# Thirty-two rows of wq through GpSimd in four transfers, each behind a quarter of gate_w, and thirty-two as quarter rows

## The chip, the cores and the metric

The kernel runs on one core of one Trainium2 chip. The metric is the device time of one execution in microseconds (us), as the median of several runs. The core has five engines with queues of their own: TensorE (PE in the profile), VectorE (DVE), ScalarE (ACT), GpSimd (POOL) and SyncE (SP), which here only issues transfers. Transfers between HBM and the on-chip memory (SBUF) are carried by 16 DMA engines, whichever engine has issued them.

## The reference, cut to what matters

Eight rows `x` (8 x 576) go through cached attention and through a small MLP, and a gate mixes the two results.

```python
def reference(A_x, A_k_cache, A_v_cache, A_wq, A_wo, B_x, B_w1, B_b1, B_w2, B_b2, gate_w):
    x = A_x                                                     # 8 x 1 x 576
    g = sigmoid((x * gate_w).sum(-1, keepdims=True))
    q = (x @ A_wq).reshape(8, 1, 32, 128)                       # A_wq is 576 x 4096
    p = softmax(q . k_cache * 128**-0.5)                        # k_cache, v_cache: 8 x 32 x 4096 x 128
    a = (p @ v_cache) @ A_wo                                    # A_wo is 4096 x 576
    b = gelu(layernorm(x) @ B_w1 + B_b1) @ B_w2 + B_b2          # B_w1 is 576 x 4608
    return g * a + (1 - g) * b
```

All operands are bf16. The two caches are 537 MB together, all of the weights some 20 MB.

## The kernel before, in words

There are 32 turns `n`, one for each batch row and group of eight heads. A turn loads 8.4 MB of keys (`load_k`, L328) and 8.4 MB of values (`load_v`, L339); each of the 128 partitions gets one run of 64 KB. VectorE multiplies the keys with the broadcast query (L500), TensorE sums the products (L511 and L183, the helper `held`), VectorE finishes the sums (L523), then come the softmax and the product with the values (L564).

An instruction is recorded by `op` or `aside` in a list for its engine, and the order of these lists is the order of execution on each engine. Waits are on semaphores. `load` (its DMA is recorded at L287) gives every transfer a semaphore of its own, on the queue of the engine that is named. Nothing plans the order: it is written out by hand.

The order of SP's queue is what sets the order of the transfers: rows 0 to 511 of `wq` (4096 KB, four rows to a partition, 32 KB each), rows 512 to 575 of `wq` as 128 half rows of 4 KB (512 KB), the first keys in two halves, `w1` in two parts, `w2` (which waits for the last matmul of the queries, `p_Q`, since it goes into the place of `wq`), the keys of turn 1 (which wait for VectorE to be done with half of turn 0's keys and for `p_up`), the values of turn 0 in two parts, and from there keys and values in turn; at the end come `wo` and the last values in pieces. ACT's queue carries `x`, `gate_w` (to eight partitions, 1152 bytes each), `b1` and `b2`. GpSimd issues no transfer: it begins with the identity matrix `ident` (L365, L368), then fills `xz`, `yz`, `ones`, `mA` and `shift`.

What happens ahead of the first turn is a small chain of its own. VectorE first makes `own`, `fine` and `shift` from `ident`, then the statistics of `x` (L397 to L405), then the dot product with `gate_w` (L407). ACT blanks three banks of PSUM (L378, for which it waits for `mA`), makes `sel_f` and `Sel` from `ident` (L390, L392), the square root (L409) and the sigmoid of the gate (L410), and spreads the last 64 columns of `x` into `xz` (L416, L417). TensorE transposes `x` (L424, six small matmuls), VectorE copies the result (L429); the same follows for the normalised `y`. Then TensorE computes the queries: two halves by four head groups by `NKT` = 5 matmuls, 40 in all (L451), for which it waits for both transfers of `wq`. ACT takes the queries out of PSUM (L454), they are broadcast (L465, L469) and turn 0's query is scaled down to its tile (L475).

The functions below are `spread`, `transposed` and `untransposed`, which the change rewrites, and the statements around them.

Of the kernel before, what the change touches and what calls it, by code (L numbers as in the profile page):

```python
# [6 lines left out]
ACT = mybir.ActivationFunctionType  # L7
ALU = mybir.AluOpType
# [4 lines left out]
B = 8  # L13
D = 576
H = 32
DH = 128
SK = 4096
F = 4608
NKF = 4
NKT = NKF + 1  # L20
# [21 lines left out]
class Stream:  # L42
# [102 lines left out]
def bass_gated_mix__mha_block_cached__mixer_channel_mlp__decode_kernel(  # L145
# [18 lines left out]
    op = S.op  # L164

    def aside(engine, fn, waits=()):
        return op(engine, fn, waits, side=1)

    def pstride(t):
        return t[tuple([slice(None)] * len(t.shape))].ap[0][0]  # L170

    def view(t, offset, shape):
        ap = []
        stride = 1
        for n in reversed(shape[1:]):
# [17 lines left out]
    KR = sb("KR", [128, RB0 + 9 * F // 2], BF16)  # L193
    VB = sb("VB", [128, NTT, DH], BF16)
    wq_sb = view(VB, 0, [128, 4, SK])
    wq_t = view(VB, 4 * SK, [128, SK // 2])
    w1_sb = view(KR, RB0, [128, 4, F])
    w1_t = view(KR, RB0 + 4 * F, [128, F // 2])
    V_AHEAD = 88
# [3 lines left out]
    p1 = sb("p1", [128, 2, CT, DH], BF16)  # L203
# [14 lines left out]
    xz = early([B, 2, 64, 2])  # L218
    yz = early([B, 2, 64, 2])
    xT_sb = early([128, NKF + 2, B])  # L220
# [52 lines left out]
    tr_ps = bank[0:2]  # L273
# [3 lines left out]
    up_ps = bank[6]  # L277
    y_ps = bank[7]
    up_bank = (qb_ps, *tr_ps)
    YT_COL = 64  # L280

    sK = nc.alloc_semaphore("sK")
    sV = nc.alloc_semaphore("sV")
# [2 lines left out]
    def load(engine, dst, src, name, waits=()):  # L286
        return op(engine, lambda e: e.dma_start(dst, src), waits, dma=(nc.alloc_semaphore(name), 16))  # L287
# [2 lines left out]
    x_flat = A_x.rearrange("b s d -> (b s) d")  # L290
    out_flat = out.rearrange("b s d -> (b s) d")

    def bcast(t):
        return bass.AP(tensor=t.tensor, offset=t.offset, ap=[[0, B], [1, D]])
# [12 lines left out]


    def kv_src(cache, n):
# [54 lines left out]
    def memset(engine, ap, value):  # L364
        return op(engine, lambda e: e.memset(ap, value))  # L365

    c_id0 = memset("gpsimd", ident[:], 0.0)
    c_id = op("gpsimd", lambda e: e.affine_select(out=ident[:], in_=ident[:], compare_op=ALU.not_equal, fill=1.0,  # L368
                                                  base=0, pattern=[[-1, 128]], channel_multiplier=1), [c_id0])
# [35 lines left out]
    t_vpe = op("vector", lambda e: e.tensor_scalar(out=stat[:, 4:5], in0=stat[:, 6:7], scalar1=1e-5, scalar2=None,  # L405
                                                   op0=ALU.add), [t])
    t_gs = op("vector", lambda e: e.tensor_tensor_reduce(out=junk, in0=x_sb, in1=gw8, scale=1.0, scalar=0.0,  # L407
                                                         op0=ALU.mult, op1=ALU.add, accum_out=stat[:, 8:9]), [ld_gw, t1])
    a_sqrt = aside("scalar", lambda e: e.activation(out=stat[:, 5:6], in_=stat[:, 4:5], func=ACT.Sqrt), [t_vpe])  # L409
    a_g = aside("scalar", lambda e: e.activation(out=stat[:, 9:10], in_=stat[:, 8:9], func=ACT.Sigmoid), [t_gs])  # L410
    G_COL, OMG_COL = 9, 10


    def spread(dst, src, waits):

        aside("scalar", lambda e: e.activation(out=dst[:, 0, :, 0], in_=src[:, 512:576], func=ACT.Copy), [*waits, c_z])  # L416
        return aside("scalar", lambda e: e.activation(out=dst[:, 1, :, 1], in_=src[:, 512:576], func=ACT.Copy))  # L417

    def transposed(src, srcz, col, waits):
        last = None  # L420
        for kt in range(NKF + 2):
            o = up_ps[:, col + kt * B:col + (kt + 1) * B]
            i = src[:, kt:NKF * 128:NKF] if kt < NKF else srcz[:, kt - NKF, :, :].rearrange("b r s -> b (r s)")
            last = aside("tensor", lambda e, o=o, i=i: e.matmul(o, lhsT=i, rhs=ident[0:B, 0:B], start=True, stop=True),  # L424
                      waits if kt == 0 else ())
        return last

    def untransposed(dst, col, waits):
        return op("vector", lambda e: e.tensor_copy(  # L429
            out=dst.rearrange("p k b -> p (k b)"), in_=up_ps[:, col:col + (NKF + 2) * B]), waits)  # L430

    v_xz = spread(xz, x_sb, [ld_x])
    p_xT = transposed(x_sb, xz, 0, [ld_x, c_id, v_xz])
    v_xT = untransposed(xT_sb, 0, [p_xT])
# [4 lines left out]
    p_yT = transposed(y_sb, yz, YT_COL, [v_yz, v_xT])  # L439
    v_yT = untransposed(yT_sb[:, :, :], YT_COL, [p_yT])  # L440

    a_Q = []
    p_Q = None
    for half in range(2):
        for h in range(4):
            for kt in range(NKT):
                o = tr_ps[half][32 * h:32 * h + B, :]
                at = (kt * SK + half * (SK // 2) if kt < NKF else NKF * SK) + h * DH
                r = bass.AP(tensor=VB, offset=at, ap=[[pstride(VB), 128], [4 * DH, 4], [1, DH]])
                xi = kt if kt < NKF else NKF + half  # L450
                p_Q = aside("tensor", lambda e, o=o, r=r, kt=kt, xi=xi: e.matmul(  # L451
                    o, lhsT=xT_sb[:, xi, :], rhs=r, start=(kt == 0), stop=(kt == NKT - 1)),
                    [v_xT, *ld_wq, *c_ps] if h == kt == half == 0 else ())
        a_Q.append(aside("scalar", lambda e, half=half: e.activation(  # L454
            out=Q4[:, half * 512:(half + 1) * 512], in_=tr_ps[half][:, :], func=ACT.Copy, scale=inv_sqrt_dh), [p_Q]))
# [443 lines left out]
```

## Time and profile before

| | |
|---|---|
| median of 3 runs | 1295.06 us (1294.94 to 1295.06) |
| span of the profiled execution, first to last instruction | 1293.1 us |
| its own time | not given apart from the span; the median is 1.96 us above the span |
| read from HBM | 556.95 MB, 431 GB/s over the span |
| busy: PE, DVE, ACT, POOL | 731.3, 851.9, 73.2, 12.7 us |
| mean granted TensorE clock | 0.837 |

Times in the profile are counted from the first instruction. A line of the chain of waits gives start, length and what ran or was waited for. A line of the timeline gives start, length, engine, source line, operation, tiles, shapes and count; in brackets stands how long the engine had been idle and what ended that. A line of the DMA issues gives the number of such issues, the size of each and the median time from issue to landing. A row of the table by windows gives, for each stretch, the busy time of the five engines with their number of instructions, the granted clock, the busy share of the 16 DMA engines and the rate in GB/s; a packet counts in the stretch in which it starts, so short stretches can show a share over one.

### The profile page before, as it was taken

The numbers are of one execution on the slowest core, as the hardware profiler recorded it, in microseconds if no ns is written. First come the engines' busy times: TensorE is split into PE (matmuls) and PEld (weight loads), VectorE is DVE, ScalarE is ACT, GpSimd is POOL, SyncE is SP. The second block draws the span as 40 slices with busy tenths as digits, with TensorE's granted clock in tenths as the row PEclk, the third lists the DMA queues.
The fourth block names the chain that finished last, engine by engine and source line by source line (L and its number), as shares of the span: only waits on it lengthen the run. The fifth ranks groups of instructions, "written<-read, shape, count | busy, mean of one in ns | idle before, by whom it ended". The sixth has DMA issues, their size and how long they took to land.

```text
span 1293.1 us, 10903 instructions
## 1 busy us (share of the span) xinstructions
PE 731.3 (57%) x4824; PEld 142.8 (11%) x3032; DVE 851.9 (66%) x1078; ACT 73.2 (6%) x164; POOL 12.7 (1%) x23
## 2 busy tenths in 40 slices
PE   3755566455556555556555556555556555557556
PEld 0211111011111011111011111001111001111003
DVE  3646667766667766667766667766668766667763
ACT  3300000000000000000000000000000000000001
POOL 0100000000000000000000000000000000000001
PEclk8978888877898787799778888877888877798878
DMA  9999999999999999999999999999999999999998
GB/s 405 427 447 424 430 442 430 438 432 430 442 428 428 444 426 430 444 428 438 434 428 442 428 428 444 428 428 444 428 438 434 428 442 428 428 444 428 428 438 356
DMA packets 11728, 557.07 MB, mean 431 GB/s; under 512 B 1448, under 2 KB 1608, under 8 KB 2120
## 3 DMA queue, kind: packets, MB, share of 16 engines
q1 hardware_dynamic: 11520, 556.93, 99.7%
q8 instruction: 5, 0.08, 0.0%
q10 hardware_dynamic: 200, 0.03, 0.0%
q14 instruction: 3, 0.02, 0.0%
HBM read 556.95 MB, written 0.01 MB: 431 GB/s over the span
## 4 chain that ended last, share of the span: by engine, by line
DMA 67%; DVE 18%; PE 9%; issue 5%; DVEq 1%; SPq 0%
DMA KR<-in_A_k_cache_dram 66%; DVE p L500 15%; PE psb L183 7%; DVE s_sb L523 2%; DMA KR<-in_A_wo_dram 2%; PE psb L511 2%; DVEq L523 0%; DVEq L137 0%; SPq L287 0%; PE psb L754 0%; DVE p L850 0%; DVEq L500 0%
## 5 line engine op out<-in xcount | busy, mean ns | idle before, releaser
L500 DVE TENSOR_TENSOR p<-KR,q_n 128x4096 bf16<-128x4096 bf16 x256 | 581.6, 2282 | 213.6 <-DMA KR<-in_A_k_cache_dram 213.6
L183 PE MATMUL psb<-p,ident 128*128 128x512 bf16 x1792 | 483.8, 415 | 0.0
L511 PE MATMUL psb<-p,ident 128*128 128x512 bf16 x256 | 112.1, 438 | 511.6 <-DVE p L500 511.6
L523 DVE TENSOR_REDUCE s_sb<-psb 128x512 f32 (+1 forms) x256 | 175.3, 685 | 106.9 <-PE psb L183 60.4
L511 PEld LDWEIGHTS psb<-p,ident 128*128 128x128 bf16 x256 | 26.1, 102 | 964.3 <-DVE p L500 963.8
L564 PE MATMUL psb<-VB,P 128*32 128x512 bf16 x1984 | 112.7, 380 | 0.0
L552 DVE TENSOR_SCALAR P<-E,own 128x256 bf16<-128x256 bf16 x256 | 53.1, 282 | 87.4 <-ACT E L549 87.4
L475 ACT ACTIVATE q_n<-q_bc 128x128 bf16<-128x128 bf16 x32 | 9.9, 310 | 871.3 <-DVE p L500 871.3
L564 PEld LDWEIGHTS psb<-VB,P 128*32 128x32 bf16 x1984 | 50.1, 97 | 47.9
L581 PE MATMUL psb<-selO,O_sb 128*128 128x8 f32 x256 | 33.9, 259 | 22.5 <-ACT O_sb L576 22.5
L581 PEld LDWEIGHTS psb<-selO,O_sb 128*128 128x128 f32 x256 | 31.0, 191 | 38.3 <-ACT O_sb L576 38.3
L576 ACT ACTIVATE O_sb<-psb 128x512 f32<-128x512 f32 x32 | 19.1, 597 | 197.9 <-PE psb L564 197.9
L571 PEld LDWEIGHTS psb<-rs,ones 128*128 128x128 f32 x64 | 12.1, 190 | 46.6 <-issue 44.4
L691 POOL TENSOR_TENSOR p<-OT_sb,fine 128x512 bf16<-128x512 bf16 (+1 forms) x4 | 5.0, 1278 | 1196.8 <-PE psb L571 1193.0
L549 ACT ACTIVATE E<-s_sb,mD 128x256 bf16<-128x256 f32 x32 | 16.0, 499 | 0.0
L540 DVE TENSOR_REDUCE mA<-s_sb 128x1 f32<-128x256 f32 x32 | 13.5, 420 | 1.1
L480 ACT ACTIVATE OT_sb<-O_n,G 128x8 bf16<-128x8 f32 x31 | 9.3, 301 | 84.3 <-DVE O_n L587 84.3
L555 DVE TENSOR_REDUCE es<-E 128x1 f32<-128x256 bf16 x32 | 13.2, 412 | 0.0
L571 PE MATMUL psb<-rs,ones 128*128 128x8 f32 x64 | 9.2, 216 | 1.3 <-DVE O_n L587 1.3
L653 PE MATMUL psb<-VB,hT_sb 128*8 128x288 bf16 x72 | 6.5, 358 | 4.7 <-POOL hT_sb L632 4.7
L556 DVE TENSOR_SCALAR rs<-own,es 128x8 f32<-128x8 f32 x32 | 7.4, 231 | 1.1
L548 DVE STREAM_TRANSPOSE mD<-mC 128x32 f32<-128x32 f32 x32 | 6.8, 212 | 1.1
(98 smaller groups left out, 125.8 us busy)
## 6 DMA issues: line engine op xcount, KB each, us to landing
KR<-in_A_k_cache_dram SPq DMA_DIRECT2D x2, 4096.0 KB, 27.2
VB<-in_A_v_cache_dram SPq DMA_DIRECT2D x1, 5376.0 KB, 27.1
VB<-in_B_w_dram SPq DMA_DIRECT2D x1, 5184.0 KB, 40.6
KR<-in_B_w_dram SPq DMA_DIRECT2D x1, 4608.0 KB, 43.2
VB<-in_A_wq_dram SPq DMA_DIRECT2D x1, 4096.0 KB, 12.5
KR<-in_A_v_cache_dram SPq DMA_DIRECT2D x1, 4096.0 KB, 22.3
VB<-in_A_v_cache_dram SPq DMA_DIRECT2D x1, 2816.0 KB, 38.4
KR<-in_A_wo_dram SPq DMA_DIRECT2D x1, 2304.0 KB, 20.7
```

What stands on the lines that cost most here:

```text
L183: return e.add_instruction(mybir.InstMatmult(name=nc.get_next_instruction_name(), engine=mybir.EngineType.PE, ins=[e.lower_ap(rhs), e.lowe ...
L500: v_mult[n, c] = op("vector", lambda e: e.tensor_tensor(out=p1[:, par, :, :], in0=k_of(), in1=qb, op=ALU.mult), [k_land[n, s], a_q[n], p_s ...
L511: fn = lambda e, r=r: e.matmul(tr_ps[par][:, :], lhsT=ident[:, :], rhs=r, start=True, stop=False)
L523: v_red[n, c] = op("vector", lambda e: e.tensor_reduce(out=s_of(), in_=tr_ps[par][:, :].rearrange("p (t c) -> p t c", c=CH), axis=AX.X, op ...
L540: t = op("vector", lambda e: e.tensor_reduce(out=mA[:, 0:1], in_=s_sb[:, :], axis=AX.X, op=ALU.max), [v_red[n, NC - 1], c_mA])
L549: a_exp[n] = op("scalar", lambda e: e.activation(out=E[:, :], in_=s_sb[:, :], func=ACT.Exp, bias=mD[:, 0:1], scale=1.0), [v_nm[n], v_P.get ...
L552: v_P[n] = op("vector", lambda e, h=h: e.tensor_scalar(out=P[:, :, h, :], in0=E[:, :].rearrange("p (q t) -> p q t", t=TQ), scalar1=own[:, ...
L555: t = op("vector", lambda e: e.tensor_reduce(out=es[:, :], in_=E[:, :], axis=AX.X, op=ALU.add), [a_exp[n]])
L564: p_pv[n] = op("tensor", lambda e, o=o, tq=tq, at=at, v=v: e.matmul(o, lhsT=P[:, tq, :, :].rearrange("p h t -> p (h t)"), rhs=v.rearrange( ...
L571: p_z[n] = op("tensor", lambda e: e.matmul(oz_ps[:, HB:2 * HB], lhsT=ones[:, :], rhs=rs[:, :], start=True, stop=True), [v_rs[n], v_norm.ge ...
L576: a_ev[n] = op("scalar", lambda e: e.activation(out=O_sb[:].rearrange("p t d -> p (t d)"), in_=o_ps[n // last][:, :], func=ACT.Copy), [p_p ...
L581: p_oz[n] = op("tensor", lambda e, tt=tt: e.matmul(o, lhsT=O_sb[:, tt, :], rhs=selO[:, tt, :], start=(tt == 0), stop=(tt == TQ - 1 and stop)),
```

## The change

Of the last 64 rows of `wq`, 32 stay on SP's queue, now as 128 quarter rows of 2 KB (`XQ` = 4, 256 KB). The other 32 (256 KB) go on GpSimd's queue in four transfers of 8 rows; a row is two pieces of 4 KB, which lie 64 elements apart in `VB` so that they stay two, and the 32 rows land in partitions 64 to 95 (transfer `j` in partitions 64 + j, 68 + j, ... 92 + j). Ahead of each of the four stands a quarter of `gate_w`, broadcast to eight partitions in two pieces of 144 bytes each, also on GpSimd's queue; ACT no longer loads `gate_w`. GpSimd issues the eight transfers after filling `mA` and before it makes `ident`.

The queries take 56 matmuls in place of 40: four of 512 columns as before, two of 256 columns for the quarter rows, and one of 512 columns over 32 partitions for the rows that GpSimd brought. The transposition of `x` has nine matmuls in place of six. The dot product with `gate_w` and its sigmoid come after the transposition of `y`; before, they came ahead of the transposition of `x`.

```diff
     wq_sb = view(VB, 0, [128, 4, SK])
-    wq_t = view(VB, 4 * SK, [128, SK // 2])
+    XQ = 4
+    XR = 64 // 2
+    XP = 64
+    wq_t = view(VB, 4 * SK, [128, SK // XQ])
+    WQB = 4 * SK + SK // XQ
+    WQH = SK // 2 + 64
...
-    gw8 = early([B, D])
+    GW = D // 8
+    gw8 = early([B, 8, GW + 8])
...
-    ld_gw = load("scalar", gw8, bcast(gate_w), "ld_gw")
...
     ld_wq = [load("sync", wq_sb, A_wq[0:512, :].rearrange("(p kt) n -> p kt n", kt=4), "ld_wqa"),
-             load("sync", wq_t, halves(A_wq), "ld_wqb")]
+             load("sync", wq_t, A_wq[512:512 + XR, :].rearrange("r (s n) -> (r s) n", s=XQ), "ld_wqb")]
...
+    c_mA = memset("gpsimd", mA[:], 0.0)
+    ld_gw = []
+    for j in range(4):
+        ld_gw.append(load("gpsimd", gw8[:, 2 * j:2 * j + 2, 0:GW],
+                          bass.AP(tensor=gate_w.tensor, offset=gate_w.offset + 2 * j * GW, ap=[[0, B], [GW, 2], [1, GW]]), f"ld_gw{j}"))
+        ld_wq.append(load(
+            "gpsimd", bass.AP(tensor=VB, offset=(XP + j) * pstride(VB) + WQB, ap=[[4 * pstride(VB), 8], [WQH, 2], [1, SK // 2]]),
+            bass.AP(tensor=A_wq.tensor, offset=A_wq.offset + (512 + XR + j) * SK, ap=[[4 * SK, 8], [SK // 2, 2], [1, SK // 2]]), f"ld_wqc{j}"))
     c_id0 = memset("gpsimd", ident[:], 0.0)
...
-    c_mA = memset("gpsimd", mA[:], 0.0)
...
+    def spread_x(waits):
+        def into(at, ap):
+            return bass.AP(tensor=xz.tensor, offset=xz.offset + at, ap=[[pstride(p1), B]] + ap)
+        xr = x_sb[:, 512:512 + XR]
+        aside("scalar", lambda e: e.activation(
+            out=into(0, [[129, XQ], [XQ, XR]]),
+            in_=bass.AP(tensor=xr.tensor, offset=xr.offset, ap=[[pstride(p1), B], [0, XQ], [1, XR]]), func=ACT.Copy), [*waits, c_z])
+        return aside("scalar", lambda e: e.activation(out=into(XQ * 128 + XP, [[1, XR]]), in_=x_sb[:, 512 + XR:576], func=ACT.Copy))
...
-            for kt in range(NKT):
-                o = tr_ps[half][32 * h:32 * h + B, :]
-                at = (kt * SK + half * (SK // 2) if kt < NKF else NKF * SK) + h * DH
-                r = bass.AP(tensor=VB, offset=at, ap=[[pstride(VB), 128], [4 * DH, 4], [1, DH]])
+            r0 = 32 * h
+            for kt in range(NKF + 3):
+                if kt < NKF:
+                    at, p0, p1_, g, o0, xi = kt * SK + half * (SK // 2), 0, 128, 4, 0, kt
+                elif kt < NKF + 2:
+                    at, p0, p1_, g, o0, xi = NKF * SK, 0, 128, 2, (kt - NKF) * 2 * DH, 2 * half + kt
+                else:
+                    at, p0, p1_, g, o0, xi = WQB + half * WQH, XP, XP + XR, 4, 0, NKF + XQ
```

More of the change, by code (lines that the diff above doesn't have):

```diff
@@ L279, in bass_gated_mix__mha_block_cached__mixer_channel_mlp__decode_kernel @@
     up_bank = (qb_ps, *tr_ps)
-    YT_COL = 64
+    YT_COL = 128
     sK = nc.alloc_semaphore("sK")
@@ L417, in spread @@
         return aside("scalar", lambda e: e.activation(out=dst[:, 1, :, 1], in_=src[:, 512:576], func=ACT.Copy))
+    def spread_x(waits):
[6 more added lines that the diff above has]
+        return aside("scalar", lambda e: e.activation(out=into(XQ * 128 + XP, [[1, XR]]), in_=x_sb[:, 512 + XR:576], func=ACT.Copy))
     def transposed(src, srcz, col, waits):
         last = None
-        for kt in range(NKF + 2):
+        n = NKF + len(srcz)
+        for kt in range(n):
             o = up_ps[:, col + kt * B:col + (kt + 1) * B]
-            i = src[:, kt:NKF * 128:NKF] if kt < NKF else srcz[:, kt - NKF, :, :].rearrange("b r s -> b (r s)")
+            i = src[:, kt:NKF * 128:NKF] if kt < NKF else srcz[kt - NKF]
             last = aside("tensor", lambda e, o=o, i=i: e.matmul(o, lhsT=i, rhs=ident[0:B, 0:B], start=True, stop=True),
@@ L426, in transposed, with untransposed @@
         return last
-    def untransposed(dst, col, waits):
+    def untransposed(dst, col, n, waits):
         return op("vector", lambda e: e.tensor_copy(
[L430 to L434, printed above, removed]
+            out=dst.rearrange("p k b -> p (k b)"), in_=up_ps[:, col:col + n * B]), waits)
+    v_xz = spread_x([ld_x])
+    p_xT = transposed(x_sb, [xz[:, i, :] for i in range(XQ + 1)], 0, [ld_x, c_id, v_xz])
+    v_xT = untransposed(xT_sb, 0, NKF + XQ + 1, [p_xT])
     t = op("vector", lambda e: e.reciprocal(out=stat[:, 7:8], in_=stat[:, 5:6]), [a_sqrt])
@@ L438, in bass_gated_mix__mha_block_cached__mixer_channel_mlp__decode_kernel @@
     v_yz = spread(yz, y_sb, [v_y])
-    p_yT = transposed(y_sb, yz, YT_COL, [v_yz, v_xT])
-    v_yT = untransposed(yT_sb[:, :, :], YT_COL, [p_yT])
+    p_yT = transposed(y_sb, [yz[:, i, :, :].rearrange("b r s -> b (r s)") for i in range(2)], YT_COL, [v_yz, v_xT])
+    v_yT = untransposed(yT_sb[:, :, :], YT_COL, NKF + 2, [p_yT])
+    t_gs = op("vector", lambda e: e.tensor_tensor_reduce(
+        out=junk.rearrange("b (s n) -> b s n", s=8), in0=x_sb.rearrange("b (s n) -> b s n", s=8), in1=gw8[:, :, 0:GW], scale=1.0, scalar=0.0,
+        op0=ALU.mult, op1=ALU.add, accum_out=stat[:, 8:9]), [*ld_gw, t1])
+    a_g = aside("scalar", lambda e: e.activation(out=stat[:, 9:10], in_=stat[:, 8:9], func=ACT.Sigmoid), [t_gs])
     a_Q = []
@@ L445, in bass_gated_mix__mha_block_cached__mixer_channel_mlp__decode_kernel @@
         for h in range(4):
-            for kt in range(NKT):
-                o = tr_ps[half][32 * h:32 * h + B, :]
-                at = (kt * SK + half * (SK // 2) if kt < NKF else NKF * SK) + h * DH
-                r = bass.AP(tensor=VB, offset=at, ap=[[pstride(VB), 128], [4 * DH, 4], [1, DH]])
-                xi = kt if kt < NKF else NKF + half
-                p_Q = aside("tensor", lambda e, o=o, r=r, kt=kt, xi=xi: e.matmul(
-                    o, lhsT=xT_sb[:, xi, :], rhs=r, start=(kt == 0), stop=(kt == NKT - 1)),
+            r0 = 32 * h
[6 more added lines that the diff above has]
+                    at, p0, p1_, g, o0, xi = WQB + half * WQH, XP, XP + XR, 4, 0, NKF + XQ
+                o = tr_ps[half][r0:r0 + B, o0:o0 + g * DH]
+                r = bass.AP(tensor=VB, offset=p0 * pstride(VB) + at + h * DH, ap=[[pstride(VB), p1_ - p0], [4 * DH, g], [1, DH]])
+                p_Q = aside("tensor", lambda e, o=o, r=r, kt=kt, xi=xi, p0=p0, p1_=p1_: e.matmul(
+                    o, lhsT=xT_sb[p0:p1_, xi, :], rhs=r, start=(kt == 0), stop=(kt == NKF + 2)),
                     [v_xT, *ld_wq, *c_ps] if h == kt == half == 0 else ())
```

9 lines of the change are left out of this document (2 added, 7 removed).

## The prediction

> **What bounds the kernel now.** I read the page from the top: busy shares, DMA queues, then the chain that ended last.
>
> ```profile
> span 1293.1 us, 10903 instructions
> DMA  9999999999999999999999999999999999999998
> q1 hardware_dynamic: 11520, 556.93, 99.7%
> q8 instruction: 5, 0.08, 0.0%
> HBM read 556.95 MB, written 0.01 MB: 431 GB/s over the span
> DMA 67%; DVE 18%; PE 9%; issue 5%; DVEq 1%; SPq 0%
> ```
>
> The 16 DMA engines are busy for practically the whole span, nearly all of it with SP's queue (q1). No compute engine comes near (VectorE 66%). The chain, in order of time, says where this queue could run dry:
>
> ```profile
> 1.67 22.61 DMA KR<-in_A_k_cache_dram
> 24.28 0.02 issue
> 24.30 2.30 DVE p L500
> ...
> 47.20 32.22 DMA KR<-in_A_k_cache_dram
> ...
> 1214.05 26.35 DMA KR<-in_A_k_cache_dram
> ```
>
> A load of 8.4 MB alone needs 8.39 / 431 = 19.5 us; turn 1's keys took 32.22 us and later ones some 26.3, so each stood 7 to 13 us behind older transfers. The queue never empties; the time is start + bytes / rate + end. The bytes stay the same here, so the change can act in three ways only: a late start, an emptied queue, or engines that end unequally. The table by windows shows start and end:
>
> ```profile
> 0.00:1.00 1.00, 0.00 (x0) 0.00 (x0) 0.00 (x0) 0.00 (x0) 0.41 (x5) 1.00 0.00 0
> 1.00:2.00 1.00, 0.00 (x0) 0.00 (x0) 0.49 (x2) 0.00 (x0) 0.82 (x4) 1.00 0.68 172
> 1288.00:1288.50 0.50, 0.50 (x24) 0.50 (x20) 0.00 (x0) 0.00 (x0) 0.00 (x0) 0.50 0.93 360
> 1288.50:1289.00 0.50, 0.48 (x18) 0.17 (x8) 0.00 (x0) 0.00 (x0) 0.00 (x0) 0.50 0.53 203
> 1289.00:1289.50 0.50, 0.03 (x4) 0.03 (x8) 0.00 (x0) 0.00 (x0) 0.00 (x0) 0.50 0.34 131
> 1289.50:1290.00 0.50, 0.50 (x20) 0.44 (x20) 0.00 (x0) 0.00 (x0) 0.00 (x0) 0.50 0.27 97
> 1290.00:1291.00 1.00, 0.83 (x24) 0.22 (x12) 0.12 (x1) 0.12 (x1) 0.00 (x0) 0.50 0.00 1
> 1265.75 23.67 DMA KR<-in_A_wo_dram
> 1289.47 1.39 PE psb L754 x27
> ```
>
> The last column but one is the DMA share. It does not drop at once: 0.93, 0.53, 0.34, 0.27, nothing. Times 16, some 8 engines still move data at 1288.75, five at 1289.25, four at 1289.75. So the engines end up to 1.5 us apart, about five of them last, and the last matmuls (L754) wait for exactly these. The share lost in those four stretches is 0.5 x (0.07 + 0.47 + 0.66 + 0.73) = 0.97 us: what a perfectly even distribution of bytes could gain at the most, 0.08%.
>
> **The change part by part.** *The first chain.* The transfers on GpSimd stand ahead of `ident`, for which VectorE, ACT and TensorE wait.
>
> ```profile
> 1.18 0.29 POOL L368 TENSOR_SCALAR_AFFINE_SELECT ident<-ident 128x128 bf16<-128x128 bf16 x1 [0.24 <-POOL ident L365]
> 0.75 0.59 ACTq L287 DMA_DIRECT2D p<-in_A_x_dram  x1
> 1.36 0.28 ACTq L287 DMA_DIRECT2D p<-in_gate_w_dram  x1
> 1.51 0.29 DVE L382 TENSOR_REDUCE own<-ident 128x8 f32<-128x128 bf16 x1 [1.51 <-POOL ident L368]
> 4.69 0.14 DVE L405 TENSOR_SCALAR stat<-stat 8x1 f32<-8x1 f32 x1
> 11.30 0.35 PE L424 MATMUL psb<-ident,p 8*128 8x8 bf16 x6 [1.26 <-ACT p L417]
> 14.71 4.45 PE L451 MATMUL psb<-VB,p 128*8 128x512 bf16 x40 [3.06 <-DMA VB<-in_A_wq_dram]
> 19.18 0.33 SPq L287 DMA_DIRECT2D VB<-in_B_w_dram  x1
> 20.91 0.31 ACT L475 ACTIVATE q_n<-q_bc 128x128 bf16<-128x128 bf16 x1
> 63.51 1.41 POOL L632 TENSOR_TENSOR hT_sb<-Q 128x288 bf16<-128x288 f32 x1 [0.55 <-ACT Q L631]
> ```
>
> No transfer on GpSimd's queue is in this trace. I bound the time it is held for each by the shortest issue on ACT, 0.28 us, and by GpSimd's longest own instruction, 1.41 us: 2.2 to 11.3 us for eight. I take 1.0 us, midway between ACT's longest issue (0.59) and that end, as the issue is the like work but GpSimd is the slower engine: 8 us. `ident` is then ready at some 9.6 us in place of 1.5. From there VectorE's run to the last statistics is the 3.3 us of before (1.51 to 4.83): 13.0. The square root (0.2), the two spreads of `x`, nine transpositions and the copy add some 1.4: 14.4 (between these points ran 7.54 to 10.28 before, with the sigmoid's table load of 1.28 between, which now comes later). The normalised `y` and its spread and transposition follow ahead of the queries on TensorE, 1.5 us as before (10.20 to 11.65): 15.9. The queries started at 14.71 before, when `wq` had landed.
>
> *The landing of wq.* The eight transfers share the engines with SP's 32 KB rows.
>
> ```profile
> b_sb<-in_B_b_dram ACTq DMA_DIRECT2D x1, 9.0 KB, 12.0
> VB<-in_A_wq_dram SPq DMA_DIRECT2D x1, 4096.0 KB, 12.5
> VB<-in_A_wq_dram SPq DMA_DIRECT2D x1, 512.0 KB, 13.4
> 1.21 0.41 SPq L287
> ```
>
> `b1` is 9 KB in 128 pieces, eight for an engine, and took 12.0 us: a small piece waits for its turn behind a big row, 12.0 / 9 = 1.3 us each with the piece that closes it. GpSimd's ring gets up to 16 pieces per engine (eight of data, eight that close). At 1.3 us the upper end is some 24 us; the lower is 14.6, where SP's last row lands now (1.21 + 13.4), as short quarter rows take turns with them. I take 17, nearer the low end, since the eight quarter rows give eight quick turns. The queries then run from 17.0; 56 matmuls at 4.45 / 40 = 0.111 us make 6.2 us: 23.2. From their end to the end of L475 stood 2.06 us (19.16 to 21.22): 25.3. The first product (L500), which waited until 24.30 for keys, starts 1.0 us later; with every upper end 7.8 us later (queries at 23.8).
>
> That is hidden by the queue:
>
> ```profile
> VB<-in_B_w_dram SPq DMA_DIRECT2D x1, 5184.0 KB, 40.6
> ```
>
> `w2`, issued at 19.18, landed at 59.8; turn 1's keys were issued at 47.20, when VectorE was done with half of turn 0's. Less 1.2 us from an issue to its first packet (0.74 to within the window from 1.00) and up to 1.8 us by which engines end apart, that cover is 9.6 us. `w2` itself waits for the queries and is issued some 4 us later, with `w1` still landing until 47. Cost 0; without the cover it would be 1.0 us, at the upper end 7.8. The moved dot product (0.75 us) and the sigmoid lie inside the wait for `wq`.
>
> *The bytes per engine.* 512 KB were spread evenly: 32 KB each. Now SP's 256 KB are (16 KB each), and GpSimd's 256 KB come in transfers of eight rows. What a transfer of eight rows does is in the stretch 1.6 to 2.6 us, in which `x` moves:
>
> ```profile
> DMA packets 32, 0.53 MB, mean 534 GB/s; under 512 B 8, under 2 KB 16, under 8 KB 16
> q10 hardware_dynamic: 16, 0.01, 7.5%
> ```
>
> ACT's queue (q10) moved eight rows of 1152 bytes, closed by eight small packets: eight engines took part. If GpSimd's do the same, and `gate_w` and `wq` alternate, all four quarters of `wq` fall on one and the same eight engines, 32 KB each, so that eight engines carry 16 KB more than before and eight 16 KB less. If the two pieces of a row are dealt to all 16, nothing shifts. 16 KB cost 16 / (431 / 16) = 0.61 us by the mean rate, 0.68 by the landings (512 KB between 13.24 and 14.61): 0.65. The queue never empties, so this lasts to the end: one half ends 0.65 earlier, the other 0.65 later. The end is that of the last engine, and the windows showed five last ones. The trace does not name them; were they drawn at random, all five would be in the relieved half once in 78 times (56 of 4368). Bounds: -0.65 and +0.65, even spread 0; I take +0.65, by the row of `x`. The Trainium skill ("DMA: Bandwidth & Descriptors", section "Why a DMA increments its semaphore by 16 and not by 1") says that a GpSimd transfer uses as many engines as the largest number up to 16 that divides its slowest dimension, consecutive ones from a cursor that moves on; with 8 that is one half for `gate_w` and the other for `wq`. The packets of `x` agree on the number; no run here shows the cursor, and by an even spread instead the sum would be 0.65 lower.
>
> *The pieces.* From 6 to 13.7 us ACT's pieces took:
>
> ```profile
> q10 hardware_dynamic: 168, 0.02, 1.8%
> ```
>
> That is 0.018 x 16 x 7.7 / 168 = 13 ns each; 16 more per engine are 0.2 us at most, 0 if they fill gaps; I take 0.15, since the engines have no gaps.
>
> **Sum**: 0 + 0.65 + 0.15 = +0.8 us on the profiled span of 1293.1, that is 1293.9; the median stands 1.96 above the span, so 1295.06 + 0.8 = 1295.9 us.
>
> **The rivals.** *It ends earlier.* The five late engines, or all but some that would end with the rest, are in the relieved half, or the instruction reads (five of 16 KB, each at least 0.61 us on one engine) fall on other engines in the longer program. For it: the halves are not random if an outside cause slows one. Against: one late engine in the loaded half is enough. 1295.06 - 0.65 + 0.15 = 1294.6.
>
> *The transfer does not do what it says.* Its 16 pieces go to 16 engines: 1295.06 + 0.15 = 1295.2. For it: every transfer has just 16 pieces. Against: the row of `x`.
>
> *Slower: GpSimd's queue makes the queries late.* One mechanism: each transfer holds GpSimd so long that `ident`, and behind it everything up to the first product, outlasts the cover of 9.6 us. With 1.0 us each the product is 1.0 us late if `wq` lands at 17; the compute chain alone ends 15.9 + 6.2 + 2.1 = 24.2, so it may slip 0.1 + 9.6 us, 1.2 us a transfer: from 2.2 us each it decides, and every further 0.1 costs 0.8. At 2.5 us the queue stands empty for 2.3 us (1298), at 3 us for 6.3 (1302). For it: nothing in the trace bounds GpSimd's issue directly. Against: it would need 1.6 times GpSimd's longest instruction. The Trainium skill (same page, section "Anatomy of one DMA — SWDGE (gpsimd) path") gives a GpSimd transfer about 2.0 us fixed, mostly waiting for the write's receipt; no run here shows it, and were all of that spent on GpSimd, the cover would just hold.
>
> **How the numbers follow.** Forecast 0.54, earlier end 0.20, even spread 0.12, late queries 0.12, and 0.02 for a gain the trace does not show. The range, 1294.3 to 1297.2, holds the first three with the bounds of their unknowns (-0.65 to +0.86, and as much again as another placing of instruction reads can do) and leaves out most of the fourth. A measurement of this kernel tells about 0.2% (2.6 us) from no change; the first three lie inside: same 0.86, slower 0.12, faster 0.02, as no distribution can gain more than 0.97.
>
> **What would show it.** `ident` near 9.6 us; queries from 16 to 19 us; turn 1's keys issued before 57 us with no gap in the DMA share after; at the end a share that falls over more than 2 us, about half the engines late, and the last `wo` landing 0.8 us later. Wrong if the DMA share drops between 57 and 70 us (late queries), if it falls within 1 us at the end (earlier end), or if the rate between turns changes.

## The result, and the profile after

The changed kernel takes 1298.8 us (median of six runs, 1298.16 to 1301.35) where the kernel before takes 1295.06 (1294.94 to 1295.23): the ratio is 1.0032 (95%: 1.0022 to 1.0043), 3.7 us or 0.29% slower. That is beyond the 0.2% (2.6 us) that the prediction took as what can be told from no change, and above the predicted range (1294.3 to 1297.2). The profiled run took 1298.33 us over a span of 1296.4, so it shows 3.3 us of the difference. The queries were late, as one rival had it, but not in the way that it gave: `ident` was not what they waited for.

The page of the changed kernel, in the lines that answer to those shown of before, hardly differs:

```profile
span 1296.4 us, 10953 instructions
DMA  9999999999999999999999999999999999999998
q1 hardware_dynamic: 11520, 556.67, 99.4%
q0 software_dynamic: 320, 0.27, 0.1%
HBM read 556.95 MB, written 0.01 MB: 430 GB/s over the span
DMA 64%; DVE 18%; PE 11%; issue 5%; DVEq 1%; POOL 1%; ACT 0%; SPq 0%; POOLq 0%
```

The bytes are the same, and the DMA engines look full in every slice of 32 us. Only PE's part in the chain is larger, 11% for 9%. The chain of waits up to the first product says where (start, length, what ran or was waited for):

```profile
1.40 0.76 POOL p L293
2.16 0.56 POOL VB L293
...
4.95 0.55 POOL p L293
5.50 14.64 DMA VB<-in_A_wq_dram
...
20.28 13.55 PE psb L478 x56
...
35.58 0.32 ACT q_n L502
...
35.98 2.30 DVE p L527
```

The transfers hold GpSimd for 0.56 us each and 0.76 for the first; the last is issued at 5.50. Its 64 KB then take 14.64 us to land, so the queries begin at 20.28 in place of 14.71. And they take 13.55 us, where 40 matmuls took 4.45. The first product starts at 35.98, 11.7 us later than before (24.30). Behind it, in the timeline:

```profile
6.53 0.29 POOL L378 TENSOR_SCALAR_AFFINE_SELECT ident<-ident 128x128 bf16<-128x128 bf16 x1 [0.24 <-POOL ident L367]
12.73 0.34 PE L442 MATMUL psb<-ident,p 8*128 8x8 bf16 x6 [1.29 <-ACT p L423]
33.85 0.33 SPq L293 DMA_DIRECT2D VB<-in_B_w_dram  x1
59.38 0.33 SPq L330 DMA_DIRECT2D KR<-in_A_k_cache_dram  x1
```

`w2` is issued at 33.85 for 19.18, and the keys of turn 1 at 59.38 for 47.20. By then SP's queue has run dry. The table by windows of the changed kernel has next to nothing there (the last column but one is the DMA share):

```profile
57.00:58.00 1.00, 1.00 (x6) 0.00 (x0) 1.00 (x2) 0.00 (x0) 0.00 (x0) 1.00 0.58 249
58.00:59.00 1.00, 0.84 (x5) 0.11 (x2) 1.00 (x1) 0.11 (x1) 0.00 (x0) 1.00 0.10 42
59.00:60.00 1.00, 0.59 (x3) 0.10 (x1) 0.95 (x2) 0.75 (x2) 0.00 (x0) 1.00 0.00 0
60.00:61.00 1.00, 1.00 (x7) 0.00 (x0) 0.00 (x0) 0.00 (x0) 0.00 (x0) 1.00 2.70 918
```

A packet counts where it starts, and one of 64 KB takes 2.4 us, so a low share alone does not show an empty queue: the kernel before, and the kernel below whose `wq` goes first, have such rows too, in this order,

```profile
58.00:59.00 1.00, 1.00 (x6) 1.00 (x6) 0.86 (x4) 0.00 (x0) 0.00 (x0) 0.88 0.15 66
59.00:60.00 1.00, 1.00 (x18) 0.40 (x15) 0.00 (x0) 0.60 (x1) 0.00 (x0) 1.00 0.00 0
```

while all of their 16 engines have a packet under way. What shows the gap is the packets under way in the trace of the changed kernel: 16 at 57.0 us, 8 at 58.0, one from 59.0 to 60.25, and 16 again at 61.25. The first engine is through with `w2` at 57.6 us and the last at 60.7. A gap of up to 3 us in a slice of 32 is what the tenths of the page round away.

### The profile page after: what moved, and what is told of

The parts are those of the page before. It is cut to its first block, busy times and chain, and to the rows that moved or that the text cites. A ratio compares the mean times of both kernels' runs of the same rounds, so it can differ in the third digit from the quotient of the medians.

```text
span 1296.4 us, 10953 instructions
## 1 busy us (share of the span) xinstructions
PE 747.2 (58%) x4843; PEld 146.4 (11%) x3051; DVE 852.3 (66%) x1078; ACT 73.3 (6%) x164; POOL 19.9 (2%) x31
## 4 chain that ended last, share of the span: by engine, by line
DMA 64%; DVE 18%; PE 11%; issue 5%; DVEq 1%; POOL 1%; ACT 0%; SPq 0%; POOLq 0%
DMA KR<-in_A_k_cache_dram 61%; DVE p L527 15%; PE psb L183 7%; DVE s_sb L550 2%; DMA KR<-in_A_wo_dram 2%; PE psb L538 2%; DMA VB<-in_A_wq_dram 1%; PE psb L478 1%; PE psb L680 1%; DVEq L550 0%; PE psb L641 0%; DVEq L137 0%; PE psb L632 0%; POOL p L293 0%; POOL VB L293 0%
## 5 line engine op out<-in xcount | busy, mean ns | idle before, releaser
L550 DVE TENSOR_REDUCE s_sb<-psb 128x512 f32 (+1 forms) x256 | 175.6, 686 | 107.3 <-PE psb L183 60.7
L478 PE MATMUL psb<-VB,p 128*8 128x512 bf16 (+2 forms) x56 | 13.5, 382 | 7.2 <-DMA VB<-in_A_wq_dram 7.2
```

Of the source, the lines that this page charges most:

```text
L478: p_Q = aside("tensor", lambda e, o=o, r=r, kt=kt, xi=xi, p0=p0, p1_=p1_: e.matmul(o, lhsT=xT_sb[p0:p1_, xi, :], rhs=r, start=(kt == 0), s ...
L550: v_red[n, c] = op("vector", lambda e: e.tensor_reduce(out=s_of(), in_=tr_ps[par][:, :].rearrange("p (t c) -> p t c", c=CH), axis=AX.X, op ...
```

## The experiments

The theory after this result: two delays add up, the late landing and slow matmuls, and both are needed, since the queue covers either alone. The matmuls are slow because of their order: behind every six that use all 128 partitions comes one that uses 32. Rivals: the late landing alone; the GpSimd queue itself (a busy software queue that slows the others); or the uneven bytes alone.

**The same matmuls in another order.** The four narrow matmuls of each half come last; nothing else changes.

```diff
-        for h in range(4):
-            r0 = 32 * h
-            for kt in range(NKF + 3):
+        for h, kt in [(h, kt) for h in range(4) for kt in range(NKF + 2)] + [(h, NKF + 2) for h in range(4)]:
+                r0 = 32 * h
```

> The changed kernel with one difference: in each half of the queries the four matmuls over 32 partitions come after the 24 over 128 partitions, in place of one behind every six. Same transfers, same 56 matmuls. Theory (the queries are late because matmuls of different head groups no longer overlap when a narrow one stands between them, and the keys of turn 1 are then issued after the queue has run empty): the queries take 6 to 8 us in place of 13.5, the keys of turn 1 are issued at 52 to 54 us in place of 59.4, the DMA share shows no gap near 57 to 60 us, and the time is 1294.4 to 1296.0 us (what is left is the uneven load of the engines, of either sign). Rival (GpSimd's transfers themselves cost the queue time, or the end is late by uneven engines alone): 1298 us as before, whatever the queries take.

Measured: 1295.74 us (1295.64 to 1296.13, ten runs) beside 1295.05; ratio 1.0006 (0.9996 to 1.0016). The timeline of this kernel:

```profile
21.05 7.68 PE L477 MATMUL psb<-VB,p 128*8 128x512 bf16 x56 [8.01 <-DMA VB<-in_A_wq_dram]
54.19 0.33 SPq L330 DMA_DIRECT2D KR<-in_A_k_cache_dram  x1
```

`wq` lands even later here, but the 56 matmuls take 7.68 us in place of 13.55, turn 1's keys are issued at 54.19, and the gap is gone (15 or more engines have a packet under way throughout). The order alone costs the changed kernel some 3 us. How, the groups of matmuls by form show (count, busy time, mean ns of one), first before:

```profile
L451 PE MATMUL psb<-VB,p 128*8 128x512 bf16 x40 | 4.4, 523 | 3.1 <-DMA VB<-in_A_wq_dram 3.1
```

then the changed kernel:

```profile
L478 PE MATMUL psb<-VB,p 128*8 128x512 bf16 x32 | 9.4, 422 | 7.2 <-DMA VB<-in_A_wq_dram 7.2
L478 PE MATMUL psb<-VB,p 128*8 128x256 bf16 x16 | 3.3, 291 | 0.0
L478 PE MATMUL psb<-VB,p 32*8 32x512 bf16 x8 | 3.2, 400 | 0.0
```

then with the narrow ones last:

```profile
L477 PE MATMUL psb<-VB,p 128*8 128x512 bf16 x32 | 6.6, 500 | 8.0 <-DMA VB<-in_A_wq_dram 8.0
L477 PE MATMUL psb<-VB,p 128*8 128x256 bf16 x16 | 3.9, 333 | 0.0
L477 PE MATMUL psb<-VB,p 32*8 32x512 bf16 x8 | 0.8, 374 | 0.0
```

A matmul of before lasts 523 ns, and 40 of them, 20.9 us if they followed one another, fill only 4.45: almost five are under way at once. In the changed kernel 32 x 422 + 16 x 291 + 8 x 400 = 21.4 us fill 13.55: 1.6 at once. With the narrow ones last it is 24.3 us in 7.68, 3.2 at once, and the stretches in which a narrow one runs shrink from 3.2 us to 0.8. The profile models the ends of matmuls, so these counts are rough; the starts of the weight loads do not depend on them. The weight loads of the changed kernel give the rhythm:

```profile
20.66 0.13 PEld L478 LDWEIGHTS psb<-VB,p 128*8 128x8 bf16 x1 [0.30 <-issue]
21.09 0.13 PEld L478 LDWEIGHTS psb<-VB,p 128*8 128x8 bf16 x1 [0.30 <-issue]
...
30.48 0.08 PEld L478 LDWEIGHTS psb<-VB,p 32*8 32x8 bf16 x1 [0.22 <-issue]
...
31.96 0.08 PEld L478 LDWEIGHTS psb<-VB,p 32*8 32x8 bf16 x1 [0.22 <-issue]
```

One group of seven takes 1.48 us (30.48 to 31.96), 0.21 us a matmul, and at the start the loads stand 0.43 us apart. The Trainium skill ("TensorEngine Tiling (Array Packing)", section "Key Properties") says that tiles of the array work in parallel, and that a change of the tiling mode drains TensorE. The runs agree with both: a narrow matmul between wide ones ends the overlap. It gives no price; here eight narrow matmuls among the wide ones cost 13.55 - 7.68 = 5.9 us more than in two groups of four, 0.7 us each. That it is a drain and not some other hindrance of the mixed order is the word of the Trainium skill; no run here separates them.

**Both delays, one at a time.** Two more kernels keep the slow order and let `wq` land early. In the first the four transfers of `wq` are issued ahead of the four of `gate_w`:

```diff
     for j in range(4):
-        ld_gw.append(load("gpsimd", gw8[:, 2 * j:2 * j + 2, 0:GW],
-                          bass.AP(tensor=gate_w.tensor, offset=gate_w.offset + 2 * j * GW, ap=[[0, B], [GW, 2], [1, GW]]), f"ld_gw{j}"))
         ld_wq.append(load(
...
+    for j in range(4):
+        ld_gw.append(load("gpsimd", gw8[:, 2 * j:2 * j + 2, 0:GW],
+                          bass.AP(tensor=gate_w.tensor, offset=gate_w.offset + 2 * j * GW, ap=[[0, B], [GW, 2], [1, GW]]), f"ld_gw{j}"))
```

> The changed kernel with GpSimd's eight transfers in another order: the four of wq first, then the four quarters of gate_w. Same bytes, same matmuls in the same order. Theory: the last piece of wq lands with SP's rows near 15 us in place of 20.1, the queries take 13.5 us as in the changed kernel, turn 1's keys are issued near 54.5 us, no gap; and as the transfers of wq now follow each other, the uneven load is gone as well if engines are dealt in turn: 1294.9 to 1295.4 us. Rival (GpSimd's transfers are the cost whatever their order): 1298 us.

In the second nothing goes through GpSimd's queue: `gate_w` is one transfer on ACT's, and the 32 rows are one on SP's, to the same partitions 64 to 95 and in the same pieces.

```diff
+    ld_gw = [load("scalar", gw8[:, :, 0:GW],
+                  bass.AP(tensor=gate_w.tensor, offset=gate_w.offset, ap=[[0, B], [GW, 8], [1, GW]]), "ld_gw")]
...
+             load("sync", bass.AP(tensor=VB, offset=XP * pstride(VB) + WQB, ap=[[pstride(VB), 32], [WQH, 2], [1, SK // 2]]),
+                  bass.AP(tensor=A_wq.tensor, offset=A_wq.offset + (512 + XR) * SK, ap=[[SK, 32], [SK // 2, 2], [1, SK // 2]]), "ld_wqc")]
...
```

> The changed kernel with the eight GpSimd transfers undone: gate_w again in one transfer on ACT's queue, the 32 rows in one transfer of 32 partitions on SP's queue. The 56 matmuls and their order stay as changed. Theory: the queries start when SP's last row has landed, near 15 us, and still take 13.5 us; turn 1's keys are issued near 54 us, still under the cover (about 56 us); time 1294.9 to 1295.4 us. So the slow matmuls alone are hidden. Rival (the slow matmuls alone are enough): 1297 us or more. Rival (GpSimd's transfers alone are enough) also 1295.1, told apart by the run with the narrow matmuls last.

Measured 1295.92 (1295.67 to 1296.19) and 1296.12 (1295.87 to 1297.44), ten runs each, beside 1295.05. In the timeline of `wq` first, then in that without GpSimd:

```profile
15.63 14.90 PE L479 MATMUL psb<-VB,p 128*8 128x512 bf16 x56 [2.61 <-DMA VB<-in_A_wq_dram]
54.93 0.33 SPq L330 DMA_DIRECT2D KR<-in_A_k_cache_dram  x1
```

```profile
16.14 13.82 PE L475 MATMUL psb<-VB,p 128*8 128x512 bf16 x56 [5.81 <-DMA VB<-in_A_wq_dram]
54.71 0.33 SPq L334 DMA_DIRECT2D KR<-in_A_k_cache_dram  x1
```

The matmuls are as slow as in the changed kernel, but they begin 4 to 5 us earlier, and there is no gap. So the table of two by two is full: early and fast (before), late and fast, early and slow are all hidden; late and slow is not. The slow matmuls appear without anything on GpSimd's queue, so that queue isn't their cause. Both times are 0.5 us or more above what was expected of a kernel without a gap; the runs with the extra rows below take that up.

**How much lateness the queue covers.** The kernel before, with the first half of its queries computed 10, 14 and 18 times more, so that only their end is late:

```diff
-    for half in range(2):
+    p_first = 10
+    for half in [0] * 10 + [0, 1]:
...
+        if p_first:
+            p_first -= 1
+            continue
```

> The kernel before, with the first half of its queries computed ten times more ahead of the real ones (200 matmuls more, about 20 us), and nothing else changed: no GpSimd transfer, no uneven load. Theory: the queries are some 20 us later, turn 1's first product some 17 us later than 24.3, turn 1's keys are issued near 64 us in place of 47.2, the queue runs empty at 58 to 60 us for some 6 to 8 us, and the time is 1301 to 1303.5 us. Rival (late queries are hidden by something further on, and GpSimd's transfers are the cost): 1295.1 us.

> The kernel before, with the first half of its queries computed 14 times more (280 matmuls more). In the run with ten times more, 240 matmuls took 16.26 us, since they speed up once TensorE is warm, and turn 1's keys were issued at 55.8 us, at the edge. Each further time adds about 1.15 us. Theory: turn 1's keys issued near 60.5 us, the queue empty for about 3 us before them, time 1298.5 to 1300 us, with no GpSimd transfer and no uneven load. Rival (a late issue of these keys is hidden further on): below 1296 us.

> The same with 18 times more (360 matmuls more). Theory: turn 1's keys issued near 65 us, time 4 to 5 us above the run with 14: 1303 to 1304.5 us, one us for each us of delay. Rival (the cost saturates or is hidden): the same time as with 14.

Measured: 1295.82 (1295.01 to 1297.37, ten runs), 1298.99 (1298.2 to 1299.43, seven) and 1303.93 (1302.92 to 1304.1, four), beside 1295.05, 1295.0 and 1295.0. The first was expected at 1301 and more, and failed: I had sized the repeats by the 0.111 us of the prediction, but the timeline of 10 more shows

```profile
14.53 16.26 PE L452 MATMUL psb<-VB,p 128*8 128x512 bf16 x240 [2.87 <-DMA VB<-in_A_wq_dram]
55.84 0.33 SPq L328 DMA_DIRECT2D KR<-in_A_k_cache_dram  x1
```

that is 0.068 us each, and 80 more of them in the step from 14 to 18 took 25.07 - 20.21 = 4.86 us, 0.061 each. With its slow first microseconds the run of 40 had given too high a price even for the wide ones. The two longer kernels, by timeline and by windows, 14 times first and then 18 times:

```profile
14.91 20.21 PE L452 MATMUL psb<-VB,p 128*8 128x512 bf16 x320 [3.29 <-DMA VB<-in_A_wq_dram]
60.14 0.33 SPq L328 DMA_DIRECT2D KR<-in_A_k_cache_dram  x1
59.00:60.00 1.00, 0.61 (x4) 0.11 (x2) 1.00 (x1) 0.35 (x1) 0.00 (x0) 1.00 0.00 0
```

```profile
14.73 25.07 PE L452 MATMUL psb<-VB,p 128*8 128x512 bf16 x400 [3.00 <-DMA VB<-in_A_wq_dram]
64.70 0.33 SPq L328 DMA_DIRECT2D KR<-in_A_k_cache_dram  x1
59.00:60.00 1.00, 0.87 (x4) 0.10 (x1) 1.00 (x3) 0.21 (x1) 0.00 (x0) 1.00 0.00 0
64.00:65.00 1.00, 0.44 (x4) 0.10 (x1) 1.00 (x2) 0.79 (x2) 0.00 (x0) 1.00 0.00 0
```

The profiled executions in which half of the engines or more ran dry lie on one line, whatever made them late; the span before is 1293.1:

```
                        keys of turn 1 issued   span     longer by   covered up to
14 times more                  60.14           1297.2      4.1          56.0
18 times more                  64.70           1302.0      8.9          55.8
the changed kernel             59.38           1296.4      3.3          56.1
the changed kernel once more   59.17           1296.6      3.5          55.7
the same, warmed (below)       57.31           1294.5      1.4          55.9
```

The last column is issue less cost: every microsecond beyond some 56 costs one. From 47.20 that is a cover of 8.8 us. Counted from the packets between 50 and 66 us, the engines stood empty for 3.2, 7.7, 2.6, 2.3 and 0.6 us each on average: most of each cost, and 0.7 to 1.2 us less than it. Where that rest goes stays open.

The profiled execution with 10 times more is not on this line. It was the slowest of its ten (1297.37), 2.5 us longer on the span than before, with these keys issued at 55.84, and its engines stood empty for only 0.3 us on average. Its trace shows uneven engines instead: from 33 us on, in the second half of the first keys, `w1` and `w2`, two of the sixteen landings come 1.5 us after the other fourteen, and the last load of all lands 0.6 us later than before on average but 2.5 us later on its last engine. What sets two engines back stays open. The changed kernel lies on the line of the repeats with no remainder for uneven bytes, which its first part does have: the sixteen landings of its first keys fall in two groups 1.2 us apart, but those of turn 1's keys, after the gap, within 1.35 us (2.03 before). So the engines start again closer together after the empty queue, and at the last load of all its landings lie within 1.74 us (1.93 before, 2.80 with the narrow ones last).

**The other half of the engines.** The narrow ones last, each transfer of `wq` ahead of its quarter of `gate_w`, and into partitions 0 to 31 (`XP` = 0).

> The changed kernel with the narrow matmuls last, and with each of GpSimd's transfers of wq ahead of its quarter of gate_w in place of behind it, into partitions 0 to 31 in place of 64 to 95. If GpSimd's transfers of eight rows are dealt to eight engines in turn, the other eight engines now carry the 32 KB each. No gap near 57 to 60 us is expected. Theory of uneven ends with late engines in both halves: again some 0.5 to 0.8 us above the kernel before, 1295.5 to 1295.9 us. If the last engines are all in the half that was loaded in the run with narrow matmuls last: 1294.3 to 1294.7 us, which would beat both kernels. If unevenness is not the cause of that run's 0.7 us: 1295.7 as there, and the landings do not fall into two groups.

Measured: 1295.52 (1294.93 to 1295.79, ten runs) beside 1295.0; ratio 1.0003 (0.9993 to 1.0013). The semaphore of the first keys shows 16 landings, which I take as one for each engine. Before, all 16 fall between 23.71 and 24.28 us. With the narrow ones last they fall in two groups, 23.29 to 23.70 and 24.52 to 25.21; here too, 23.18 to 24.03 and 24.34 to 24.89; with `wq` first there is one group, 24.54 to 24.97. So alternating transfers do load one half of the engines more, as the prediction took it, and four `wq` transfers in a row spread. The moving cursor of the Trainium skill ("DMA: Bandwidth & Descriptors", section "Why a DMA increments its semaphore by 16 and not by 1"), which the prediction cited, agrees with that. The cost is in the spread and not in the mean: with the narrow ones last and in the other half, the 16 landings of the first keys are 0.19 us later than before on average (24.10 for 23.91). At the last load of all they are 0.28 and 0.14 us later on average, but 0.73 and 0.41 on the last engine, which is the 0.7 and 0.4 us of the spans. Neither half gives a gain, as it would if all late engines stood in one half: the rival "it ends earlier" did not come about with either.

**Where the extra of the early kernels comes from.** The kernel before, with 32 rows of `wq` loaded once more (256 KB, into a place that nothing reads), once as 128 pieces of 2 KB into 128 partitions, once as 64 pieces of 4 KB into partitions 64 to 95.

> The kernel before, with 32 rows of wq loaded once more at the end of SP's transfers of wq, as 128 quarter rows of 2 KB into 128 partitions of a place that nothing reads (256 KB more, 16 KB for each engine). Price of the bytes: 0.6 us, so 1295.5 to 1295.8 us.

> The same 256 KB once more, but into 32 partitions (64 to 95), 64 pieces of 4 KB, as in the run without GpSimd's transfers. Theory (pieces that all engines write into the same 32 partitions are slower than pieces spread over 128): 0.4 to 0.7 us above the run with 128 partitions, 1296.0 to 1296.4 us, which would account for the 0.9 to 1.1 us of the two runs that had neither a gap nor an uneven load. Rival (the 32 partitions do not matter): the same time as with 128.

Measured: 1295.81 (1295.6 to 1296.1) and 1296.54 (1296.4 to 1297.52), ten runs each, beside 1294.99. The first is at the upper end of its range and the second 0.14 us above its own. The same bytes cost 0.73 us more in 32 partitions than in 128. The DMA issues of the two, in that order, show these rows (count, size, median us to landing):

```profile
VB<-in_A_wq_dram SPq DMA_DIRECT2D x1, 256.0 KB, 13.4
```

```profile
VB<-in_A_wq_dram SPq DMA_DIRECT2D x1, 256.0 KB, 14.7
```

They land 1.3 us later after their issue, and the delay is there at the first keys already, whose 16 landings come at 25.52 us on average in place of 24.59. A cost of this size accounts for most of the 1.07 us of the kernel without GpSimd, which has no bytes more, only these pieces on the same queue (first keys at 25.11 on average, 23.91 before). It does not settle the 0.87 us of `wq` first. There the first keys land 0.80 us later than before on average (24.71), but only 0.19 later with the narrow ones last, where the same pieces go to the same partitions through the same queue, with a quarter of `gate_w` ahead of each. What makes four transfers of `wq` in a row dearer, and why a write to few partitions takes longer, stays open.

**The slow start.** The changed kernel, with 70 matmuls of `ident` with itself on TensorE while it waits for `wq`:

```diff
+    for i in range(70):
+        aside("tensor", lambda e: e.matmul(oz_ps[:, 0:128], lhsT=ident[:, :], rhs=ident[:, :], start=True, stop=True),
+              [c_id] if i == 0 else ())
```

> The changed kernel with 70 matmuls of the identity with itself (128 columns each, into a bank that is overwritten later) on TensorE between the transposition of y and the queries, while TensorE waits for wq. Theory (the queries of the changed kernel begin on a slow TensorE, and how long that lasts moves turn 1's keys and with them the end): the queries take some 12 us in place of 13.5, turn 1's keys are issued near 57.7 us in place of 59.3, the time is 1296.6 to 1297.6 us, and the runs agree better than within the 3 us of the changed kernel. Rival (the slow begin has no part in it): 1298.8 us with the same scatter.

Measured: 1296.96 (1295.83 to 1298.58, ten runs) beside 1294.99, ratio 1.0016 (1.0006 to 1.0025). In its timeline:

```profile
13.01 5.67 PE L465 MATMUL psb<-ident 128*128 128x128 bf16 x70
20.38 11.91 PE L482 MATMUL psb<-VB,p 128*8 128x512 bf16 x56 [1.70 <-DMA VB<-in_A_wq_dram]
20.35 0.98 PEld L482 LDWEIGHTS psb<-VB,p 128*8 128x8 bf16 x6 [1.84 <-issue]
21.55 0.08 PEld L482 LDWEIGHTS psb<-VB,p 32*8 32x8 bf16 x1 [0.22 <-issue]
57.31 0.33 SPq L330 DMA_DIRECT2D KR<-in_A_k_cache_dram  x1
```

The very first group now has the rhythm of the later ones, and the 56 matmuls take 11.91 us, eight groups of 1.48. So 1.6 us of the 13.55 were a slow start that earlier work on TensorE removes. The granted clock seems to contradict this: in the changed kernel's windows it reads 1.00 (the last but two) while the loads stand 0.43 us apart:

```profile
20.00:21.00 1.00, 0.72 (x2) 0.24 (x3) 0.00 (x0) 0.00 (x0) 0.00 (x0) 1.00 1.06 459
```

But the first record of the clock in this trace begins only at 23.8 us, at 1.00, and that is where the steps go from 0.43 to 0.21 us; the windows ahead of it read 1.00 with no record to go by. The warmed kernel has its first record at 16.4 us, among the 70 matmuls, and the kernel before at 17.8, three microseconds into its queries. So the two agree. How long the slow part lasts differs from run to run: 3.5 us here, 4.1 without GpSimd, 6.5 with `wq` first and 4.9 in the changed kernel once more (next part), and in these four the queries take 11.7 to 11.8 us plus half of that time: 13.55, 13.82, 14.90 and 14.21.

The Trainium skill ("TensorE: Matmul & The Clock Gate", section "Part 1: The HAM clock gate") states a clock of half speed after an idle window; the steps of 0.43 and 0.21 us, their change by earlier matmuls and the first records of the clock agree with it.

**The changed kernel once more**, on the chip of the longer repeats and the other half.

> The changed kernel as it is, on the chip of these runs. Theory: 1298 to 1301 us, with turn 1's keys issued at 59 to 62 us; the spread from run to run comes from when they are issued. Rival (its 3.7 us belong to the chip of the first runs): near 1295.7 us.

Measured: 1298.85 (1298.43 to 1301.87, five runs) beside 1295.0; ratio 1.0038 (1.0024 to 1.0052). The result holds. Its runs scatter by 3.4 us, those of before by 0.5; warming TensorE did not narrow that (2.75 us), and what does it is open.

## Why the prediction was wrong, step by step

*The bound: right.* Start, bytes and end set the time. In the changed kernel it was the emptied queue, one of the three ways that the prediction named. A way that it did not name, the same bytes going slower, showed in two of the experiments (without GpSimd, and with `wq` first).

*The first chain on GpSimd: over-sized, and harmless for `ident`.* "1.0 us" a transfer was 0.56 to 0.76; `ident` was made at 6.53 to 6.82, not 9.6, and `y` was transposed at 13.07, not 15.9. This part, on which the rival of late queries hung, was faster than forecast. What the issue of eight transfers did set is when the last of them went out, 5.50.

*The landing of wq: inside its bounds, but late.* Taken 17, measured 20.14, bounds 14.6 to 24. The four big transfers had a median of 10.8 us and the last took 14.64: three had landed by 14.99 us and SP's own rows by 15.16, the fourth at 20.14. It is late by its place in the queue and not by its bytes: with `wq` first the eighth transfer, a quarter of `gate_w` of 2.2 KB, lands at 20.11, and all of `wq` by 15.54. The choice near the low end cost 3.3 us: the eight quick turns that the quarter rows were to give did not bring the landing forward, and which packets stood ahead of the last piece was not taken apart.

*The queries: the step that failed.* "56 matmuls at 4.45 / 40 = 0.111 us make 6.2 us." They took 13.55. The division spread the time of 40 overlapping matmuls of one shape over 56 of three shapes in a mixed order. Before, their durations, as the profile models them, summed to 4.7 times their stretch, so an overlap was there to be read, and nothing asked whether the narrow matmul keeps it. Of the 7.4 us, 5.9 are the order (13.55 against 7.68); the other 1.5 are there with the narrow ones last too, where 56 matmuls start 4.3 us slow and not 3.1 as the 40 before, and no run splits them. No bound was given for this term, so the stated upper end of 7.8 us for the first product fell short of the measured 11.7.

*The cover: right in kind, 0.8 us too large.* Given as 9.6 us, it is 8.8 (56.0 less 47.20). The rival's price, one microsecond for each beyond it, holds over the range from 1.4 to 8.9 us, within some 0.3. With `q_n` 10.6 us after the forecast (3.3 from the landing, 7.3 from the matmuls), turn 1's keys were issued 59.38 - 56.0 = 3.4 us too late: the 3.3 measured on the span. By the forecast landing of 17 the slow matmuls alone would have ended at 30.6, 3.3 us earlier: just at the edge.

*The uneven bytes: right, but for a kernel without a gap.* 0.65 and 0.15 were forecast; without the gap the changed transfers cost 0.69 us (narrow ones last) and 0.52 (the other half), and the landings show that as engines that end apart. In the changed kernel itself no such cost is left on its line. The late engines were read off the DMA shares as eight, five and four at 1288.75, 1289.25 and 1289.75 us; by the packets under way they are ten, six and six, which leaves the argument as it is. So the sum of +0.8 fits the changed transfers with another order of matmuls. The cost of writing 32 partitions (0.73 us on SP's queue), which the sum left out, did not show in these two kernels; that it did not is luck.

*The chances.* Late queries had 0.12, tied to a price on GpSimd of 2.2 us or more. That its sign was named (a DMA share that drops between 57 and 70 us) made it easy to find, but two other ways into the same rival, a late landing and slower queries, were not counted into it: the first was taken at one value inside wide bounds, the second at one value with none.

## What to carry to other kernels

A duration divided by a count is a price only for the same mix in the same order: where durations sum to several times their stretch, ask what an added shape does to the overlap. Where a cover hides several delays in a row, add up their upper ends before calling them free; here either of two delays alone would have stayed hidden, and both together cost 3.3 us on the span. The order of eight matmuls was worth more than all of the transfers, and no version tried beat the kernel before (the best were 1295.52 and 1295.74).

## What the runs showed of the hardware that I had not expected

- One matmul over 32 partitions behind every six over 128, in four column groups: 0.24 us a matmul (13.55 / 56, slow start included); with the narrow ones last 0.14 (7.68 / 56); wide ones alone, warm, 0.061.
- A transfer of 64 KB in eight rows on GpSimd's queue was issued in 0.56 us and landed 10.8 us later in the median, up to 14.64, beside a full queue of 32 KB rows. The eighth transfer of that queue landed at 19.9 to 20.9 us in all six executions with that queue, whether it was 64 KB or 2.2 KB; the first six had landed by 15.8.
- 256 KB into 32 partitions cost 0.73 us more than into 128, on SP's queue.
- The first 3.1 to 6.5 us of the queries run at half the pace (0.43 for 0.21 us between weight loads), up to the first record of the granted clock (17.8 us before, 23.8 in the changed kernel, 22.1 with `wq` first). A window ahead of that record reads 1.00 all the same.
- A DMA share of 0.00 in a window of 1 us (59 to 60 us with `wq` first) stood beside 16 engines with a packet of 64 KB under way.
